# A fused attention and gated-MLP kernel on one core: the first phase's hand-written order is replaced, with 55 in place of 78 identity products in it

## The chip, the cores and the metric

The kernel runs on one core of a Trainium2 chip. A core has TensorE (matrix products), VectorE, ScalarE, GpSimd (POOL in the rows) and SyncE, whose queue here issues all DMA loads and stores. The metric is the device time of one execution in microseconds.

## The reference

Eight batches of eight heads have 576 positions of width 64. Keys and values are averaged over groups of 8 positions, so each head attends to 72 pooled keys. The result, with all heads side by side, is the input x of 4608 tokens of width 512 for a normalised gated MLP of inner width 1536. All arrays are float32 for the kernel (the weights arrive as float64).

```python
k_p = k.reshape(B, H, Sp, pool, D).mean(axis=3)      # pool = 8, Sp = 72
v_p = v.reshape(B, H, Sp, pool, D).mean(axis=3)
scores = scale * np.matmul(q, k_p.transpose(0, 1, 3, 2))
attn = np.exp(scores - max);  attn = attn / (sum + 1e-09)
x = (attn @ v_p), heads side by side                  # 4608 x 512
xn = x / sqrt(mean(x * x) + 1e-06) * rms_g
g = xn @ w_gate;  val = xn @ w_val                    # 512 -> 1536
out = (g * sigmoid(g) * val) @ w_out                  # 1536 -> 512
```

## The kernel before

**Tiling.** The tokens go in nine blocks of 512. Each factor of a large product is split in a high part and a rest, and three products are added (high × high, low × high, high × low), so one gate tile (f, one of 12 slices of 128 inner columns) takes 12 TensorE products of 512 columns, its value tile another 12, and its share of the output product 12 more.

**Two phases.** `later_phase` (from block 1 on) and `first_phase` each run a hand-written table of steps, `LATER` and `ORDER`. No planner stands behind it: the scheduler is in manual mode, and every engine and SyncE's queue take their instructions in the order in which the table names them. A step that waits holds up whatever follows on the same engine. `first_phase` loads and converts all weights, does the attention of batches 0 and 1, and block 0 of the MLP.

**The steps of the first phase** carry a letter and digits (base 36); after a colon stand the PSUM banks:

- `k`, `q`, `v` load keys, queries, values of a batch and a pair of heads; `K` (L360) and `V` (L369) pool them on VectorE. `S` is the scores (20 small products, L412), `M` the maximum (L378), `E` five exponentials on ScalarE (L390), `R` the inverse of the sums (L396), `N` the normalising on POOL (L402), `T` the transposes on TensorE (L472), `C` or `D` their copies out on VectorE (L478) or ScalarE, `A` the product with the values (L494), `X` or `Y` the copy of x on VectorE (L516) or ScalarE. `k`, `q`, `v` to `Y` have batch, pair and head or half as digits: T122 is batch 1, pair 2, third transpose group.
- For the norm of batch 0: `Z` squares (L521), `J` joins on POOL (L545), `P` sums over channels on TensorE (L587), `p` the total (L592), `r` the root (ScalarE, L599, with a table load), `s` its reciprocal (L602), `B` the spread over partitions (TensorE, L611), `H` the scaling (L619). `I`, `x`, `y` make block 0's scaled x (L827), its high part (ScalarE, L832) and its low part xl (VectorE, L837).
- Weights come in chunks, `l` to `w`, in the order that `CHUNKS` gives (chunk 8 is gate and value of f = 4, chunk c of f = 6, e of f = 7): `l` loads (L261), `a` takes the absolute value (ScalarE, L272), `b` shifts (L276), `c` ors in the low word (L280), `d` the sign (L284), on VectorE, `h` casts the high part (ScalarE, L298), `w` takes the rest (VectorE, L302). Raw loads of neighbouring slices alternate between two spaces (line 256), so the load of chunk c waits until chunk 8's `d` has read it.
- `g`, `e` are the gate and value products (L848), `G` the silu (ScalarE), `F` its product with the value (VectorE, L860), `i`, `j` the high part (ScalarE, L870) and the low part (VectorE, L878), `o` the output product (L892). `t` makes the part of block 1's x, `Q` squares batch 1's x.
- `z` is the identity product: `warm(n)` (L962) multiplies the identity with itself n times, and nobody reads the result. It stands between steps of TensorE, as in `zg:0` (16 of them) or `za:2` (10). In the trace such a product shows as two rows.

**Stages.** Four buffers (`st0` to `st3`) take the raw halves of the weight chunks, the transposes' copies, squares and later tiles. The string `STAGES` names for each tile, in the order of the program, which of the four it takes; a tile waits until the last reader of the former one is done.

Of the kernel before, what the change touches and what calls it, by code (L numbers as in the profile page):

```python
# [49 lines left out]


ORDER = """
k01 zg:0 q00 k00 K00 v00 q01 v01 q02 k02 v03 v02 k03 K01 za:7 S00:01 M000 M001 q03 l3 l1 E000 z2:7 S01:45 M010 E010
M011 E011 E001 V00 K02 zf:7 S02:06 R000 N000 R011 N011 z4:7 T011:1 T000:5 V03 M020 R001 N001 K03 z2:7 S03:32 M021 E020
R020 N020 C011 M030 C000 T001:1 C001 E021 R021 N021 R010 N010 M031 V01 E030 R030 N030 T002:0 D002 T020:4 C020 V02 a1
b1 z2:7 A000:1 Z00 A001:0 Z01 Y001 T021:5 z2:7 T022:0 E031 D022 Y000 R031 D021 z4:7 T030:4 c1 l0 a0 b0 d1 c0 z1:7
A020:1 Y020 Z20 D030 T010:0 D010 l2 a2 l5 k10 q10 l4 v10 z2:7 T012:1 C012 N031 T032:5 z2:7 A021:0 Y021 h1 Z21 J02 d0
T031:4 C031 w1 C032 A010:1 Z10 h0 K10 w0 z2:7 A011:0 Z11 A030:5 S10:46 M100 M101 a5 Y011 Y010 Z30 a3 E100 b2 b3 R100
b5 c2 A031:0 Z31 J01 P01:7 za:2 P03 p E101 c3 R101 N101 r0 s0 za:2 B00:1 a4 Y031 k11 X030 V10 N100 z2:2 T100:0 D100 I1
x1 c5 I0 x0 I3 I2 d3 d5 d2 y1 z4:2 T102:0 D102 x3 y0 T101:5 D101 h5 x2 y2 z4:2 A101:1 A100:0 y3 b4 g0:2 e0:3 h2 Y100  # L60
Y101 h3 w3 w2 l6 q11 v11 l7 a7 b7 l9 K11 S11:01 c4 G0 F0 d4 c7 a6 b6 d7 i0 h4 B01:4 w5 c6 H01 h7 j0 d6 g1:2 e1:3 G1 a9
F1 b9 w4 w7 c9 o0:4567 g2:2 lb l8 a8 b8 la ld i1 Q10 j1 o1 d9 e2:3 c8 d8 ab h6 G2 M111 bb M110 h8 w6 g3:2 V11 E110
R110 N110 T110:0 h9 w9 E111 F2 R111 N111 T111:1 i2 ad D110 k12 K12 v12 lc cb aa db D111 hb bd cd j2 dd ba w8 ca T112:0
e3:3 o2 G3 F3 ac hd D112 i3 wb da bc g4:2 e4:3 q12 lf lh le af bf k13 cf j3 A111:0 df ha wa wd V12 G4 F4 cc ae hf i4
ah wf A110:1 Y110 o3 g5:2 j4 o4 e5:3 be dc bh ch ce dh hc wc de G5 F5 v13 lj lg li aj Y111 bj Q11 J11 S12:01 M121 i5
j5 hh wh he M120 we cj dj g6:2 e6:3 ag G6 bg cg q13 ll lm o5 g7:2 E120 R120 N120 E121 R121 N121 F6 dg T120:1 hj i6 ai
bi V13 wj j6 ci al hg T121:0 C121 D120 K13 bl wg e7:3 lk ln G7 F7 T122:0 D122 o6 cl di dl i7 hi j7 A121:1 A120:0 Y120
wi X121 am bm ak bk g8:2 S13:01 M130 ck M131 hl wl E130 G8 R130 N130 dk E131 R131 N131 Q12 J12 an bn o7 e8:3 g9:2 F8
i8 j8 cn dn cm dm T130:1 T131:0 C130 hk G9 e9:3 o8 F9 wk D131 hn hm wm T132:0 D132 ga:2 A130:0 lp ap bp wn lo i9 j9
X130 cp dp A131:1 X131 Ga Q13 J13 ao ea:3 o9 Fa ia bo co do P10:0 r1 s1 ja hp wp gb:2 B10:0 H10 ho wo B11:1 H11 eb:3  # L70
oa Gb Fb t0 ib jb k20 v20 q20 t2 t3 t1 K20 V20 ob
"""


# [125 lines left out]
lo89 mo89 hi8a lo8a mo8a hi8b lo8b mo8b ev80 ev81 st80 st81 ev82 ev83 st82 st83  # L200
"""
STAGES = """
0123012301203102303213003213231201233102131221302121032130213231031323132113210302330113003210203210320120323013031201
01302321210231010102310312313032310321
"""
EXP_SCALE = 1.0 / (POOL * float(np.sqrt(D)))
# [790 lines left out]
```

## Time and profile before

| | us |
|---|---|
| median of 3 runs (1003.81 to 1010.04) | 1007.66 |
| profiled execution | 1005.87 |
| its span | 1004.0 |
| TensorE busy | 982.4 (98%) |
| VectorE busy | 672.7 (67%) |
| ScalarE busy | 475.6 (47%) |
| POOL busy | 201.7 (20%) |

The profile is of one execution, and the time of an instruction is read from its row: start, duration, engine, line, operation, tiles, and in brackets the idle time before it with what ended it. TensorE's clock is granted in full (1.00) or in part; its mean over this span is 0.997. Rows of consecutive instructions overlap a little, as one is started before the other's last writes are out.

### The profile page before, as it was taken

How to read it: one execution, taken by the hardware profiler on the slowest of the kernel's cores; microseconds unless marked ns; L12 is line 12 of the kernel's file. 1: busy time of each engine (PE TensorE's matmuls, PEld its weight loads, DVE VectorE, ACT ScalarE, POOL GpSimd, SP SyncE). 2: the span in 40 equal slices, each digit the busy share in tenths (PEclk: the TensorE clock that was granted, in tenths of full speed). 3: DMA queues.
4: the chain of work that ended last, by engine and by line, in shares of the span. 5: the costliest groups of instructions: out<-in, count | busy, mean ns of one | idle time of the engine just before them, and what ended most of it. 6: DMA issues, size and time to landing. Idle time of an engine off the chain costs nothing.

```text
span 1004.0 us, 13974 instructions
## 1 busy us (share of the span) xinstructions
PE 982.4 (98%) x4914; PEld 776.0 (77%) x4914; DVE 672.7 (67%) x1107; ACT 475.6 (47%) x865; POOL 201.7 (20%) x201
## 2 busy tenths in 40 slices
PE   9999999999899999899999999999999999999998
PEld 8877778777677778687777778788777787888886
DVE  6899977866776958467777788754567744444442
ACT  5867674655656644346575454632254321111221
POOL 2200111566545568201111020000010000000000
PEclk9999999999899999999999999999999999999999
DMA  9545511888666751668786661665565225545411
GB/s 280 175 148 197 197 43 60 251 248 257 210 204 213 227 184 63 212 187 237 205 232 188 200 191 48 200 191 154 149 177 140 73 95 153 152 147 147 148 42 42
DMA packets 115797, 167.35 MB, mean 167 GB/s; under 512 B 9552, under 2 KB 70992, under 8 KB 114448
## 3 DMA queue, kind: packets, MB, share of 16 engines
q1 hardware_dynamic: 115728, 166.47, 54.4%
q8 instruction: 39, 0.64, 0.3%
q14 instruction: 30, 0.25, 0.1%
HBM read 121.21 MB, written 45.22 MB: 166 GB/s over the span
## 4 chain that ended last, share of the span: by engine, by line
PE 79%; DVE 8%; ACT 4%; issue 3%; POOL 2%; DMA 2%; SPq 0%; ACTq 0%; POOLq 0%; DVEq 0%
PE po L892 25%; PE py L800 20%; PE px L800 15%; PE psg L848 12%; PE psx L494 3%; PE pss L412 3%; DMA main<-kT 1%; DVE hl L878 1%; ACT prob L390 1%; POOL wsum L709 1%; DMA sum<-wt 1%; DVE wt L284 1%; DVE act L860 1%; DVE xp L774 1%; POOL wt L722 1%
## 5 line engine op out<-in xcount | busy, mean ns | idle before, releaser
L892 PE MATMUL po<-w,hh 128*128 128x512 f32 x864 | 225.6, 390 | 0.0
L800 PE MATMUL py<-xp,wp 128*128 128x512 f32 x864 | 221.7, 392 | 1.6 <-DVE u L954 1.6
L800 PEld LDWEIGHTS py<-xp,wp 128*128 128x128 f32 x864 | 160.9, 188 | 39.4 <-DVE u L954 2.6
L892 PEld LDWEIGHTS po<-w,hh 128*128 128x128 f32 x864 | 161.9, 188 | 35.3 <-issue 1.2
L848 PE MATMUL psg<-xh,w 128*128 128x512 f32 x576 | 183.4, 400 | 4.3 <-DVE act L860 4.1
L800 PE MATMUL px<-xp,wp 128*128 128x512 f32 x648 | 166.4, 392 | 2.0 <-ACT act L949 1.9
L800 PEld LDWEIGHTS px<-xp,wp 128*128 128x128 f32 x648 | 120.4, 188 | 31.5 <-ACT act L949 3.4
L848 PEld LDWEIGHTS psg<-xh,w 128*128 128x128 f32 x576 | 106.6, 190 | 34.9 <-issue 6.7
L892 PE MATMUL po<-w,hl 128*128 128x512 f32 x432 | 125.0, 398 | 2.5 <-DVE hl L878 2.3
L848 PE MATMUL psg<-xl,w 128*128 128x512 f32 x288 | 113.3, 395 | 0.1
L443 POOL TENSOR_TENSOR prob<-prob,sm 128x360 f32<-128x360 f32 x48 | 40.5, 843 | 332.4 <-DVE sm L439 306.4
L892 PEld LDWEIGHTS po<-w,hl 128*128 128x128 f32 x432 | 79.0, 188 | 26.7 <-DVE hl L878 5.9
L878 DVE TENSOR_TENSOR hl<-act,hh 128x512 fp32r<-128x512 f32 x72 | 57.7, 801 | 30.9 <-ACT hh L870 28.4
L947 ACT COPY hb<-px 128x512 f32<-128x512 f32 x36 | 21.1, 587 | 110.5 <-PE px L800 110.5
L870 ACT CAST hh<-act 128x512 fp32r<-128x512 f32 x72 | 44.8, 622 | 58.7 <-DVE act L860 31.0
L950 DVE TENSOR_TENSOR u<-u,py 128x512 f32<-128x512 f32 x36 | 24.6, 683 | 67.6 <-PE py L800 67.6
L952 ACT ACTIVATE hb<-hb 128x512 f32<-128x512 f32 x36 | 22.7, 632 | 95.6 <-DVE hb L951 95.5
L848 PEld LDWEIGHTS psg<-xl,w 128*128 128x128 f32 x288 | 54.6, 190 | 12.7 <-DVE xl L837 0.9
L433 ACT ACT_TABLE_LOAD x38 | 48.8, 1283 | 0.7
L878 DVE TENSOR_TENSOR hl<-hb,hh 128x512 fp32r<-128x512 f32 x36 | 24.7, 687 | 34.3 <-ACT hh L870 34.3
L870 ACT CAST hh<-hb 128x512 fp32r<-128x512 f32 x36 | 22.4, 622 | 51.1 <-PE po L892 51.1
L722 POOL TENSOR_TENSOR wt<-wsum,wt 128x256 fp32r<-128x256 f32 x48 | 39.2, 820 | 35.2 <-ACT wt L718 35.2
(135 smaller groups left out, 1312.0 us busy)
## 6 DMA issues: line engine op xcount, KB each, us to landing
wp<-sum SPq DMA_DIRECT2D x144, 256.0 KB
wp<-blocks SPq DMA_DIRECT2D x108, 256.0 KB
sum<-wt SPq DMA_DIRECT2D x48, 256.0 KB
blocks<-w SPq DMA_DIRECT2D x24, 512.0 KB
wx<-w SPq DMA_DIRECT2D x10, 1024.0 KB
v<-vN SPq DMA_DIRECT2D x32, 288.0 KB
out<-o SPq DMA_DIRECT2D x36, 256.0 KB
wx<-w SPq DMA_DIRECT2D x16, 512.0 KB
```

Of the source, the lines that this page charges most:

```text
L412: nc.tensor.matmul(s["ps", h][:, t * SP:(t + 1) * SP], s["q"][r, o:o + P], s["pk"][r, :], start=True, stop=True)
L433: nc.scalar.activation(l_pr(h), l_pr(h), AF.Exp, scale=EXP_SCALE)
L443: nc.gpsimd.tensor_tensor(l_pr(h), l_pr(h), sm[:, :, None].broadcast_to([P, len(OFFS2), SP]), ALU.mult)
L494: nc.tensor.matmul(ps[r, :n], s["pv"][:, r], x, start=True, stop=True)
L722: nc.gpsimd.tensor_sub(y[:, 1], place(f, f"T{k}"), y[:, 0].bitcast(F32))
L800: nc.tensor.matmul(ps[:, :NB], w[:, a, c, :], x[:, b, c, :], start=j == 0 and not more, stop=j == len(todo) - 1, skip_group_check=more)
L848: nc.tensor.matmul(ps[:, :NB], w[:, c, cols], x[c], start=(j == 0), stop=(j == len(todo) - 1))
L870: nc.scalar.copy(a, act_in(i, f))
L878: eng.tensor_sub(l, act_in(i, f), hh[i, f].bitcast(F32))
L892: nc.tensor.matmul(po[i, t], x[i, f][:, t * P:(t + 1) * P], w, start=(f == 0 and k == 0), stop=(f == NF - 1 and k == 2))
L950: u3=lambda i, f: V.tensor_add(u3(i), u2(i), st["Y", i, f, 3]),
L952: sw=lambda i, f: S_.activation(later(i, f), later(i, f), AF.Silu),
```

## The change

The table `ORDER` is written anew, with the same steps but for the identity products (16 at the start and 55 after them, in place of 16 and 78), and the copies out of the transposes and of x divided slightly differently over VectorE and ScalarE. The first 20 characters of `STAGES` give other buffers to the tiles from chunk b on. `LATER` and all functions stay as they are. The first line of the table and the string:

```diff
 ORDER = """
-k01 zg:0 q00 k00 K00 v00 q01 v01 q02 k02 v03 v02 k03 K01 za:7 S00:01 M000 M001 q03 l3 l1 E000 z2:7 S01:45 M010 E010
...
+zg:0 k01 q00 k00 v00 K00 S00:01 K01 q01 v01 z1:7 S01:45 q02 k02 v03 v02 k03 q03 l3 M000 E000 l1 l0 V00 M010 M011 E011
...
 STAGES = """
-0123012301203102303213003213231201233102131221302121032130213231031323132113210302330113003210203210320120323013031201
+0123023102310232131203103213231201233102131221302121032130213231031323132113210302330113003210203210320120323013031201
```

TensorE around the sum over channels (psr, lines of `P`) and the spread of the root (psb), before:

```order
L494 MATMUL psx_3_1_498<-own_254 64x288 x2
L587 MATMUL psr_503<-one,own_127 116x1 x5
L962 MATMUL warm<-ident 128x128 x10
L587 MATMUL psr_503<-one,own_254 116x1 x5
L962 MATMUL warm<-ident 128x128 x10
L611 MATMUL psb_0_550<-ident,r_536 128x116 x3
```

and in the changed kernel:

```order
L494 MATMUL psx_3_1_457<-own_246 64x288 x2
L962 MATMUL warm<-ident 128x128 x2
L587 MATMUL psr_469<-one,own_127 116x1 x5
L962 MATMUL warm<-ident 128x128 x10
L587 MATMUL psr_469<-one,own_246 116x1 x5
L962 MATMUL warm<-ident 128x128 x13
L611 MATMUL psb_0_528<-ident,r_511 128x116 x3
```

Thirteen identity products stand ahead of the spread in place of ten, and two more ahead of the first sum.

VectorE from the reciprocal of the root (r) to the first low part of block 0's x (xl); pv and pk are pooled values and keys of batch 1, xraw is x, wt a weight chunk under conversion. Before:

```order
L602 RECIPROCAL r_536<-r_536 116x5
L516 COPY xraw_346<-psx_3_0_460 128x288
L369 TENSOR_REDUCE pv_0_562<-v_0_412 72x128
L827 SCALAR_TENSOR_TENSOR xraw_346<-xraw_346,gcol,psb_0_550 128x512
L280 SCALAR_TENSOR_TENSOR wt_480<-wx_404,wt_480 128x512
L827 SCALAR_TENSOR_TENSOR xraw_346<-xraw_346,gcol,psb_0_550 128x512 x3
L284 SCALAR_TENSOR_TENSOR wt_485<-wx_158,wt_485 128x512
L284 SCALAR_TENSOR_TENSOR wt_480<-wx_404,wt_480 128x512
L284 SCALAR_TENSOR_TENSOR wt_402<-wx_400,wt_402 128x1024
L837 TENSOR_TENSOR xl_1_587<-xraw_346,xh_1_576 128x512
```

and in the changed kernel:

```order
L602 RECIPROCAL r_511<-r_511 116x5
L369 TENSOR_REDUCE pv_0_547<-v_0_545 72x128
L276 TENSOR_SCALAR wt_549<-wt_549 128x1024
L360 TENSOR_REDUCE pk_1_554<-k_1_552 128x72
L827 SCALAR_TENSOR_TENSOR xraw_338<-xraw_338,gcol,psb_0_528 128x512 x4
L276 TENSOR_SCALAR wt_567<-wt_567 128x1024
L837 TENSOR_TENSOR xl_0_591<-xraw_338,xh_0_589 128x512
```

The four steps of x stand in one run; one low word and three signs have gone from between them and xl, and a pool of keys and two shifts have come in ahead of xl.

TensorE at the transposes of batch 1, pair 2 (pst_2) and tile f = 7 (psg_7_0 gate, psg_7_1 value; po is the output product of f = 6), before:

```order
L848 MATMUL psg_7_0_1181<-xl_3_625,w_7_1124 128x512
L472 MATMUL pst_2_0_1213<-ident,prob 72x128 x4
L472 MATMUL pst_2_1_1235<-ident,prob 72x128 x4
L848 MATMUL psg_7_1_1246<-xh_0_580,w_7_1124 128x512 x2
...
L848 MATMUL psg_7_1_1246<-xl_3_625,w_7_1124 128x512
L472 MATMUL pst_2_2_1266<-ident,prob 72x128 x2
```

and in the changed kernel:

```order
L848 MATMUL psg_7_1_1170<-xl_3_605,w_7_1061 128x512
L472 MATMUL pst_2_1_1216<-ident,prob 72x128 x4
L472 MATMUL pst_2_0_1228<-ident,prob 72x128 x4
L472 MATMUL pst_2_2_1234<-ident,prob 72x128 x2
L892 MATMUL po_0_716<-w_6_1105,hl_6_1200 128x512
```

All three groups of transposes stand behind the value tile of f = 7, and the second group goes first.

Elsewhere in the table, among others: N110 (the normalising of batch 1, pair 1, first head) stands ahead of o1, e2 and g3, and the transposes T110, T111 and T112 behind g3; M130 and M131 stand next to each other; the second spread (B01) stands ahead of g0 in place of behind S11; and the sign step `d8` stands behind K12, close ahead of the load `lc`:

```
before:  ... e2:3 c8 d8 ab h6 G2 ... D110 k12 K12 v12 lc cb ...
after:   ... db G2 E110 R110 N110 o1 e2:3 g3:2 c8 F2 h9 E111 R111 V11 k12 w9 K12 d8 v12 lc ...
```

## Rows read from the trace of the kernel before

**Rows 1.** The page's account of the chain that ended last: shares of the span by engine.

```profile
PE 79%; DVE 8%; ACT 4%; issue 3%; POOL 2%; DMA 2%; SPq 0%; ACTq 0%; POOLq 0%; DVEq 0%
```

**Rows 2.** Busy time in stretches of 25 us: stretch, its length, then busy time and count of instructions of TensorE, its weight loads, VectorE, ScalarE and POOL, the granted clock, the share of the DMA engines and GB/s.

```profile
50.00:75.00 25.00, 24.59 (x120) 19.06 (x119) 24.90 (x37) 16.28 (x24) 0.00 (x0) 1.00 0.41 152
75.00:100.00 25.00, 23.21 (x109) 18.10 (x108) 23.68 (x37) 17.62 (x41) 2.07 (x2) 1.00 0.59 197
100.00:125.00 25.00, 23.27 (x123) 18.53 (x123) 23.88 (x35) 16.80 (x40) 3.56 (x3) 1.00 0.52 199
```

**Rows 3.** TensorE's timeline where it stood idle in the first phase, and its last row (start, duration, instruction, in brackets the idle time before it and what ended it).

```profile
63.08 1.17 PE L892 MATMUL po<-w,hl 128*128 128x512 f32 x4 [0.16 <-DVE hl L878]
...
78.11 0.63 PE L472 MATMUL pst<-ident,prob 128*72 128x128 f32 x4 [0.92 <-POOL prob L402]
79.61 0.85 PE L472 MATMUL pst<-ident,prob 128*72 128x128 f32 x6 [0.88 <-POOL prob L402]
...
121.41 0.41 PE L472 MATMUL pst<-ident,prob 128*72 128x128 f32 x2 [1.74 <-DVE pt L478]
...
140.02 0.63 PE L472 MATMUL pst<-ident,prob 128*72 128x128 f32 x4 [0.70 <-POOL prob L402]
140.90 0.74 PE L848 MATMUL psg<-xh,w 128*128 128x512 f32 x2 [0.25 <-DVE act L860]
...
169.58 0.61 PE L892 MATMUL po<-w,hh 128*128 128x512 f32 x2
```

**Rows 4.** TensorE's timeline, the opening and the way to the second gate tile.

```profile
18.68 0.61 PE L962 MATMUL warm<-ident 128*128 128x128 f32 x4
20.12 1.34 PE L412 MATMUL pss<-own,main 64*128 64x72 f32 x20 [0.84 <-DVE own L360]
...
36.32 1.18 PE L587 MATMUL psr<-one,own 128*116 128x1 f32 x10 [0.17 <-POOL own L545]
...
40.61 2.48 PE L962 MATMUL warm<-ident 128*128 128x128 f32 x20
42.93 1.22 PE L611 MATMUL psb<-ident,r 116*128 116x116 f32 x10
...
49.18 2.14 PE L848 MATMUL psg<-xh,w 128*128 128x512 f32 x8
...
52.65 0.63 PE L848 MATMUL psg<-xh,w 128*128 128x512 f32 x2
...
55.70 1.34 PE L412 MATMUL pss<-pk,q 64*128 64x72 f32 x20
56.97 0.43 PE L611 MATMUL psb<-ident,r 116*128 116x64 f32 x2
57.21 0.70 PE L848 MATMUL psg<-xh,w 128*128 128x512 f32 x2
```

**Rows 5.** VectorE's timeline: opening, root, x and its low part, and two places further on.

```profile
19.27 0.75 DVE L360 TENSOR_REDUCE own<-main 128x72 f32<-128x576 f32 x1 [0.48 <-DMA main<-kT]
...
40.79 0.17 DVE L592 TENSOR_REDUCE total<-psr 116x5 f32<-116x10 f32 x1 [0.42 <-PE psr L587]
...
42.40 1.21 DVE L369 TENSOR_REDUCE pv<-v 72x128 f32<-72x1024 f32 x1
44.18 0.75 DVE L827 SCALAR_TENSOR_TENSOR xraw<-xraw,gcol,psb 128x512 f32<-128x512 f32 x1 [0.57 <-PE psb L611]
...
45.45 2.06 DVE L827 SCALAR_TENSOR_TENSOR xraw<-xraw,gcol,psb 128x512 f32<-128x512 f32 x3
47.42 2.42 DVE L284 SCALAR_TENSOR_TENSOR wt<-wx,wt 128x512 uint32<-128x512 uint32 x3
49.76 2.49 DVE L837 TENSOR_TENSOR xl<-xraw,xh 128x512 fp32r<-128x512 f32 x4
52.17 0.69 DVE L276 TENSOR_SCALAR wt<-wt 128x1024 uint32<-128x1024 uint32 x1
...
88.22 1.03 DVE L276 TENSOR_SCALAR wt<-wt 128x1024 uint32<-128x1024 uint32 x2
...
141.53 0.69 DVE L878 TENSOR_TENSOR hl<-act,hh 128x512 fp32r<-128x512 f32 x1 [0.69 <-ACT hh L870]
```

**Rows 6.** ScalarE's timeline around copies and weight chunks, and the issues of loads on SyncE's queue (SPq).

```profile
79.12 0.59 ACT L478 COPY pt<-pst 72x512 f32<-72x512 f32 x1
...
84.87 1.16 ACT L272 ACTIVATE wt<-wx 128x1024 f32<-128x1024 f32 x1 [0.40 <-DVE w L302]
...
93.26 1.16 ACT L272 ACTIVATE wt<-wx 128x1024 f32<-128x1024 f32 x1 [1.97 <-DMA wx<-w]
...
75.89 0.33 SPq L261 DMA_DIRECT2D wx<-w  x1
...
76.75 11.96 SPq L261 DMA_DIRECT2D wx<-w  x3
```

**Rows 7.** TensorE and VectorE around 251 us, and the busy time of two microseconds from 254 us (columns as in rows 2).

```profile
254.49 1.22 PE L848 MATMUL psg<-xh,w 128*128 128x512 f32 x2 [2.91 <-DVE act L860]
...
259.91 0.90 PE L494 MATMUL psx<-pt,pv 72*64 72x256 f32 x4
...
246.92 6.92 DVE L578 SCALAR_TENSOR_TENSOR xraw<-xraw,gcol,acc 128x288 f32<-128x288 f32 x8
...
254.00:256.00 2.00, 1.51 (x4) 1.24 (x5) 1.97 (x5) 1.52 (x2) 0.00 (x0) 0.50 0.96 283
```

More of the change, by code (lines that the diff above doesn't have):

```diff
@@ L52 @@
 ORDER = """
-k01 zg:0 q00 k00 K00 v00 q01 v01 q02 k02 v03 v02 k03 K01 za:7 S00:01 M000 M001 q03 l3 l1 E000 z2:7 S01:45 M010 E010
[L54 to L71, printed above, removed]
+zg:0 k01 q00 k00 v00 K00 S00:01 K01 q01 v01 z1:7 S01:45 q02 k02 v03 v02 k03 q03 l3 M000 E000 l1 l0 V00 M010 M011 E011
@@ new lines @@
+l2 l5 k10 q10 R000 N000 M001 E001 K02 zf:7 S02:06 E010 T000:5 R011 N011 T011:1 V03 M020 E020 K03 z1:7 S03:32 R001 M021
+E021 N001 T002:0 C011 M030 R020 N020 E030 C000 T001:1 C001 D002 M031 E031 R030 R021 N021 z4:7 T020:4 C020 V02 N030
+R010 N010 z1:7 A001:0 Z01 Y001 R031 N031 A000:1 Z00 V01 a1 b1 c1 z1:7 T021:5 T022:0 D022 Y000 D021 a0 b0 T030:4 D030
+A020:1 Z20 Y020 T010:0 D010 a2 c0 d0 z2:7 T012:1 C012 d1 A021:0 Z21 T031:4 C031 K10 T032:5 C032 Y021 h1 w1 h0 w0
+A010:1 Z10 Y010 A011:0 Z11 l4 S10:46 M100 b2 M101 Y011 a5 b5 c2 A030:5 Z30 A031:0 J02 J01 a3 b3 Z31 z2:2 P01:7 za:2
@@ new lines @@
+P03 p X030 E100 R100 c3 E101 R101 N101 d3 r0 s0 zd:2 B00:1 Y031 N100 z2:2 T100:0 v10 V10 a4 b4 k11 K11 I2 l6 q11 v11
+D100 I0 I1 I3 a6 b6 z3:2 T102:0 D102 T101:5 D101 B01:4 A100:0 x0 y0 x1 y1 x2 y2 Y100 x3 y3 h3 w3 A101:1 Y101 g0:2 e0:3
+G0 d2 h2 c6 c5 l7 a7 w2 d6 h6 F0 i0 c4 b7 d4 h4 H01 j0 c7 S11:01 M111 d7 g1:2 e1:3 h7 G1 w4 d5 F1 o0:4567 g2:2 Q10 w7
+h5 w5 i1 j1 l9 a9 lb l8 la ld a8 w6 b9 c9 ab bb M110 cb b8 d9 db G2 E110 R110 N110 o1 e2:3 g3:2 c8 F2 h9 E111 R111 V11
+k12 w9 K12 d8 v12 lc q12 aa i2 j2 ba T110:0 D110 ad bd h8 w8 N111 T111:1 D111 ca cd da T112:0 D112 G3 e3:3 o2 g4:2 F3
@@ new lines @@
+dd ac bc cc hb hd wd wb A110:1 A111:0 Y110 i3 j3 Y111 e4:3 lf af bf V12 cf G4 ha wa o3 g5:2 lh le k13 F4 ae i4 dc j4
+o4 v13 df ah bh be ce K13 de ch hc wc e5:3 G5 F5 dh he we lj lg li S12:01 M121 i5 M120 j5 q13 ll lm ag bg hh wh cg dg
+hf ai bi wf aj bj cj g6:2 G6 e6:3 F6 o5 dj g7:2 e7:3 E121 R121 N121 E120 al i6 j6 bl hj wj hg Q11 R120 N120 cl J11
+T121:0 C121 G7 F7 wg ci di T120:1 D120 T122:0 D122 lk ln ak bk o6 ck dl i7 am j7 A121:1 X121 V13 bm A120:0 Y120 hi wi
+hl g8:2 G8 o7 Q12 J12 S13:01 M130 wl M131 dk E130 cm R130 E131 R131 an bn cn hk e8:3 F8 g9:2 dn hn wn i8 j8 N131
@@ L72 @@
+T131:0 D131 N130 T130:1 C130 e9:3 o8 T132:0 G9 dm hm D132 F9 i9 wk ga:2 A130:0 wm X130 A131:1 X131 lp ap lo ao bo Q13
+j9 bp ea:3 o9 Ga cp dp Fa ia hp k20 v20 K20 ja co do J13 P10:0 r1 s1 gb:2 B10:0 H10 B11:1 Gb ho H11 eb:3 wo oa Fb ib
+jb wp t2 t0 t3 t1 V20 ob q20
 """
```

## The prediction

> **What bounds the kernel now.** I read the chain of waits first [rows 1]: TensorE is 79% of it, VectorE 8%. Time is won where TensorE stands idle, or is busy with something that nobody reads. The change touches only the first phase, whose last out product on TensorE ends at 170.1 (169.58 and on [rows 3]). So the second view is TensorE's busy time in stretches of 25 us [rows 2]: from 50 to 125 us it lacks 0.4, 1.8 and 1.7 of them, with VectorE at 24.90, 23.68 and 23.88 of 25. Both are nearly full, and single places decide. The third view, TensorE's timeline with its gaps, names them [rows 3]: 0.16 (63.08), 0.92 (78.11), 0.88 (79.61), 1.74 (121.41), 0.70 (140.02), 0.25 (140.90). Up to about 50 us TensorE hides its idle time under identity products; there I follow the chain that lets the first gate product start, on TensorE [rows 4] and VectorE [rows 5].
>
> The profiled execution took 1005.87 us, 1.79 under the median of 1007.66. The sum is made against the first. Rows overlap by some 0.08; a cost in a queue is taken from start to start.
>
> **Opening: no gain.** The loads that go first keep their order, and VectorE's pool of k03 starts at 19.27, when its load lands [rows 5]; S03 starts at 20.12 [rows 4]. The chain behind it (exponentials, transposes, squares, J01) keeps its instructions on their engines, so I carry P01 over at 36.3.
>
> **Root and spread: +0.65.** 10 products stood between the sums P03 and the spread B00, at 2.32 (40.61 to 42.93 [rows 4]); now 13, 3 × 0.232 = 0.70. On VectorE X030 (0.35), two inverses (0.6), a low and a sign (1.2) now stand between the total p, at 40.79 [rows 5], and the reciprocal s0, which comes at about 43.0 and so not behind the products. B00 starts at 43.6 in place of 42.93.
>
> **First gate product (A): −1.45.** VectorE waited 0.57 for B00 and ran, from 44.18, an x (0.66) and a low (0.60), from 45.45 three more x, from 47.42 three signs (2.34) and from 49.76 four xl (0.60 each), the last ending at 52.2 [rows 5]. In the changed order V10 (1.13, as at 42.40), a shift (0.60, as at 52.17) and K11 (0.66, the size of the row at 19.27) fill the time from 43.05, so the four x begin at 45.45: 4 × 0.66, a shift 0.60, four xl at 0.60, end 51.1. That is 1.1 earlier though x begins later, because the low and the signs no longer stand between. The gate's 12 products had waited on the xl from inside: 49.18 to 52.65, 3.5, where the value's 12 took 3.0 up to S11 at 55.70. Now 51.1 + 0.3 for the last xl product + 3.0 + S11's 1.27 = 55.7. B01's 0.24, ahead of the next gate before (57.21), goes ahead of the first. The weights of that next gate end on VectorE behind a half w, a sign, two lows and a w (512 words 0.60, 1024 words 1.13): 51.1 + 0.60 + 1.13 + 1.13 + 0.60 + 1.13 = 55.7. So g1 starts at 55.75: −1.45.
>
> **T110 and T111 (B): −1.5.** They waited 0.92 and 0.88 for POOL's normalise [rows 3]. Now o1, e2 and g3, 12 products each and over 8 us together, run between the normalise of N110 and T110. Both gaps go, and so does the 0.16, since j0 stands ahead of S11's maximum. Next late is T112, which needs T110's bank copied out by ScalarE (D110, 0.59 as at 79.12 [rows 6]): I leave 0.45. 0.16 + 0.92 + 0.88 − 0.45 = 1.5. Bounds of the new wait: 0, and the 1.74 that a transpose waited for such a copy.
>
> **T122 (C): −1.44.** It waited 1.74 for C121, behind conversions on VectorE [rows 3]. Now all three transposes stand behind e7, 12 products later, and I leave 0.3: the copy less the transposes beside it. Bounds again 0 and 1.74.
>
> **T131 and e9 (D): +0.15.** 0.70 and 0.25 before. M130 and M131 stand together and the order of the transposes turns: N131 comes 0.75 late by the queues, N130 0.35. ScalarE loads two tables fewer, as the exponentials of both heads stand side by side; its idle time covers that.
>
> Sum on TensorE: **−4.25**, its part of the phase ends near 165.9.
>
> **Loads and POOL.** Chunks lb to lo and batch 1's squares take other stage buffers. The only load that the queue issues clearly later is lc (below). The later phase keeps its order; its first POOL step, a sum of weights that block 3 wants, shares its buffer with v20 before and with a square now. It can start earlier; I cost it at nothing, its cover being the time until block 3.
>
> **What is carried to the end.** At 251.58 TensorE waits 2.91 for VectorE (a value product behind eight scale steps that start at 246.92), and the clock then stands at 0.50 from 254 on [rows 7]. That wait ends on VectorE, so what counts there is VectorE's lead. Behind the last value product VectorE has Fb, jb, wp, the pairs of t and V20: jb waits about 0.69 for ScalarE's hi, as at 141.53 [rows 5], which a t covered before. With 0.1 to 0.2 from wp in K20's place the lead is 3.4 there and 4.25 on TensorE. I take **−3.8**, between them. 1005.87 − 3.8 = 1002.1; by medians 1007.66 − 3.8 = **1003.9**. With B's and C's waits 0.8 off either way: 1002.2 to 1005.2.
>
> **The rivals.**
>
> *The clock falls in the opening.* Two products (18.68) and a gap of 0.84 stood ahead of S03 [rows 4], and four more ahead of the transposes before. Now one stands there, and with S02 and two transposes done by 17.4 TensorE has nothing until 20.0: 2.6. Rows: gaps of 0.84 to 1.74 left the clock at 1.00, one of 2.91 halved it [rows 3, 7], and 2.6 is nearer to that. Price: S03's 20 rows (1.34) at half speed, +1.3, up to +2.5 with the transposes behind them; they feed ScalarE's queue, which hands it on to J01. Then 1005.2 to 1006.4. The Trainium skill, "TensorE: Matmul & The Clock Gate", Part 1, says "the default state is throttled, and activity releases the throttle"; by that rule products that nobody reads are worth something, and the sum would be this rival's 1005.8. The trace agrees at 254.
>
> *A load that comes too late* (slower). Load lc goes into the space that chunk 8 leaves with its sign step d8. Before, d8 stood early, and lc was issued at 75.89 [rows 6]. Now d8 stands behind K12 on VectorE: about 78.2. Its data are wanted by ac on ScalarE and then by bc on VectorE, which stood at 88.22 [rows 5] and comes at about 84.95 by A, B and its place. One landing is bounded from below by le's: the last of three issues (76.75 and 11.96 on), so at 88.4, read at 93.26 after a wait for the transfer: 4.9. lc at 83.1 is in time. From above: lc itself, read at 84.87 after an issue at 75.89, 9.0. Then lc lands at 87.2, ac ends at 88.25, VectorE's queue moves by 3.3 and o3 with it. A stall of 3.3 is longer than the one that halved the clock, which cost 2.7 more (12 products from 254.49 to 259.91 in place of 2.7). −3.8 + 3.3 + 2.7 = +2.2: **1009.9**. It decides from 6 us of landing on.
>
> *The gap at 251 closes.* If later transfers find their place earlier, both the 2.91 and the slow 2.7 go: 998.3. Against it: both engines move together.
>
> *It is swallowed.* If VectorE's steps up to 246.92 hang on transfers and not on its own queue, the gap grows by what was won: 1007.7. For it: the second batch's loads share the time. Against it: the scale steps run without a break, 6.92 for eight [rows 7].
>
> **Chances.** Forecast 0.50, clock 0.20, late load 0.13, closed gap 0.07, swallowed 0.10. The range leaves out most of the late load and half of the closed gap: **998.5 to 1009.5**. A measurement of this kernel tells some 1%, 10 us, from no change: faster by that 0.06 (the closed gap and more behind it), slower 0.04 (the late load and a second stall), the same 0.90.
>
> **What would show it.** In the changed profile: four x in one row from 45.4, the last xl ending at 51.1, g1 at 55.75 (A); no gaps ahead of T110 and T111, e3 at 77.2 in place of 80.22 (B); under 0.5 ahead of T122 (C); the phase's last out product ending near 165.9, and the wait of about 2.9 near 247. A granted clock under 1.00 from 6 to 24 us shows the first rival, ScalarE waiting for a transfer near 85 us the second. I am wrong in the main if the first gate's chain is not shorter, or if T112 and T122 wait as long as T110 and T121 did.

## The result, and the profile after

| us | before | after |
|---|---|---|
| median of 9 runs each (lowest to highest) | 1005.82 (1003.21 to 1010.04) | 1014.19 (1012.27 to 1016.59) |
| profiled execution, its span | 1005.87, 1004.0 | 1015.59, 1013.6 |
| TensorE busy | 982.4 | 981.2 |
| POOL busy | 201.7 | 211.1 |

The ratio is 1.009, with an interval of 1.0072 to 1.0108: the change makes the kernel 8.4 us **slower**, 0.9%. The forecast was 1003.9, and the time lies outside the range too. Three single executions among all the runs took far longer than the others of their kernel (1103.66 to 2498.27), and medians and ratios leave them out. One row of the small table is odd: POOL executes the same work and is busy for 9.4 us more.

The chain of waits after, as shares of the whole span, and then some of its pieces from 72 to 93 us (start, duration, instruction):

```profile
PE 79%; DVE 8%; ACT 4%; POOL 3%; DMA 3%; issue 2%; SPq 1%; ACTq 0%; POOLq 0%; DVEq 0%
...
76.15 9.55 POOL prob L402
...
85.74 1.49 PE pst L472 x6
87.23 4.86 PE psg L848 x12
```

The shares hardly move against [rows 1]. The pieces name the loss: one POOL step, the normalise N111, takes 9.55. POOL's timeline of both kernels, first before, then after:

```profile
78.77 0.79 POOL L402 TENSOR_TENSOR prob<-prob,mx 128x360 f32<-128x360 f32 x1 [0.72 <-ACT hh L870]
```

```profile
74.14 1.58 POOL L402 TENSOR_TENSOR prob<-prob,mx 128x360 f32<-128x360 f32 x1 [28.75 <-ACT w L298]
76.15 9.54 POOL L402 TENSOR_TENSOR prob<-prob,mx 128x360 f32<-128x360 f32 x1 [0.43 <-DVE mx L397]
...
146.42 2.27 POOL L402 TENSOR_TENSOR prob<-prob,mx 128x360 f32<-128x360 f32 x2 [5.45 <-ACT wt L272]
```

The same instruction on the same shapes takes 0.79 in one order and 9.54 in the other. TensorE's timeline after shows who pays:

```profile
56.48 0.73 PE L848 MATMUL psg<-xh,w 128*128 128x512 f32 x2
...
62.06 1.07 PE L892 MATMUL po<-w,hl 128*128 128x512 f32 x4
...
75.77 0.63 PE L472 MATMUL pst<-ident,prob 128*72 128x128 f32 x4
85.74 1.49 PE L472 MATMUL pst<-ident,prob 128*72 128x128 f32 x6 [9.33 <-POOL prob L402]
86.88 1.20 PE L848 MATMUL psg<-xh,w 128*128 128x512 f32 x2
...
91.93 1.07 PE L892 MATMUL po<-w,hl 128*128 128x512 f32 x4
...
128.33 0.92 PE L472 MATMUL pst<-ident,prob 128*72 128x128 f32 x6 [0.28 <-POOL prob L402]
...
147.55 0.63 PE L472 MATMUL pst<-ident,prob 128*72 128x128 f32 x4 [1.35 <-POOL prob L402]
148.75 0.63 PE L472 MATMUL pst<-ident,prob 128*72 128x128 f32 x4 [0.56 <-POOL prob L402]
...
180.35 1.34 PE L412 MATMUL pss<-pk,q 64*128 64x72 f32 x20
...
266.04 1.22 PE L848 MATMUL psg<-xh,w 128*128 128x512 f32 x2 [2.90 <-DVE act L860]
```

The gap ahead of T110 (0.92 in [rows 3]) is gone, and that ahead of T111 is 9.33 in place of 0.88. Then the clock is down. Two microseconds behind the stall (columns as in [rows 2]):

```profile
88.00:90.00 2.00, 2.00 (x6) 1.53 (x5) 0.00 (x0) 1.99 (x3) 0.00 (x0) 0.50 0.97 400
```

At 0.50, the lower of its two levels, the 12 products of e3 take 5.05 (86.88 to 91.93); before they took 2.85 (80.22 to 83.07), so the stall costs 2.2 more behind itself, and another 0.5 in the six transposes ahead of them (1.14 for 0.61 from start to start). VectorE, which was full in [rows 2], waits too; its timeline at the first xl and over the stall:

```profile
48.94 2.55 DVE L837 TENSOR_TENSOR xl<-xraw,xh 128x512 fp32r<-128x512 f32 x4 [0.30 <-ACT xh L832]
...
75.81 0.19 DVE L397 RECIPROCAL mx<-mx 128x5 f32<-128x5 f32 x1
75.92 1.17 DVE L369 TENSOR_REDUCE pv<-v 72x128 f32<-72x1024 f32 x1
77.01 0.68 DVE L302 TENSOR_TENSOR w<-wt,w 128x512 fp32r<-128x512 f32 x1
77.61 0.74 DVE L360 TENSOR_REDUCE pk<-k 128x72 f32<-128x576 f32 x1
78.28 1.21 DVE L284 SCALAR_TENSOR_TENSOR wt<-wx,wt 128x1024 uint32<-128x1024 uint32 x1
79.41 0.68 DVE L878 TENSOR_TENSOR hl<-act,hh 128x512 fp32r<-128x512 f32 x1
80.01 1.02 DVE L276 TENSOR_SCALAR wt<-wt 128x1024 uint32<-128x1024 uint32 x2
80.95 1.22 DVE L302 TENSOR_TENSOR w<-wt,w 128x1024 fp32r<-128x1024 f32 x1
82.08 1.82 DVE L280 SCALAR_TENSOR_TENSOR wt<-wx,wt 128x1024 uint32<-128x1024 uint32 x2
83.82 1.21 DVE L284 SCALAR_TENSOR_TENSOR wt<-wx,wt 128x1024 uint32<-128x1024 uint32 x1
92.20 0.69 DVE L860 TENSOR_TENSOR act<-act,psg 128x512 f32<-128x512 f32 x1 [7.17 <-PE psg L848]
```

The inverse that N111 needs is done at 76.0. From 75.92 to 85.03 VectorE runs eleven steps without a break, and N111 ends at 85.69, 0.66 after the last of them. The row doesn't show when POOL worked; its end suggests that most of its 0.79 of work was done when VectorE had stopped.

### The profile page after: what moved, and what is told of

It is laid out like the page before. It is cut to its first block, busy times and chain, and to the rows that moved or that the text cites. A ratio compares the mean times of both kernels' runs of the same rounds, so it can differ in the third digit from the quotient of the medians.

```text
span 1013.6 us, 13874 instructions
## 1 busy us (share of the span) xinstructions
PE 981.2 (97%) x4868; PEld 774.3 (76%) x4868; DVE 676.7 (67%) x1107; ACT 472.4 (47%) x863; POOL 211.1 (21%) x201
## 4 chain that ended last, share of the span: by engine, by line
PE 79%; DVE 8%; ACT 4%; POOL 3%; DMA 3%; issue 2%; SPq 1%; ACTq 0%; POOLq 0%; DVEq 0%
PE po L892 25%; PE py L800 19%; PE px L800 14%; PE psg L848 13%; PE psx L494 3%; PE pss L412 3%; POOL prob L402 1%; DMA v<-vN 1%; DMA out<-o 1%; DVE hl L878 1%; DVE w L302 1%; ACT prob L390 1%; DVE wt L280 1%; DVE act L860 1%; DVE wt L284 1%
## 5 line engine op out<-in xcount | busy, mean ns | idle before, releaser
L722 POOL TENSOR_TENSOR wt<-wsum,wt 128x256 fp32r<-128x256 f32 x48 | 42.2, 882 | 36.2 <-ACT wt L718 36.1
L860 DVE TENSOR_TENSOR act<-act,psg 128x512 f32<-128x512 f32 x36 | 24.6, 683 | 33.5 <-PE psg L848 31.1
```

Source lines behind the costliest of these rows:

```text
L722: nc.gpsimd.tensor_sub(y[:, 1], place(f, f"T{k}"), y[:, 0].bitcast(F32))
L860: nc.vector.tensor_mul(t, t, ps[:, :NB])
```

## The experiments

Theory from here on, **port**: a POOL step cannot run beside certain VectorE steps, and an unbroken run of them keeps it out. The Trainium skill, "SBUF — State Buffer", Who interferes with whom, states such a rule: the two engines share one pair of ports, a VectorE step with two inputs in SBUF (the on-chip memory that holds the tiles) "contends with a GpSimd instruction that reads SBUF", and a `tensor_reduce` does not. The rival, **input**: N111 waits for something else that the profile doesn't show, so moving VectorE's steps would not help.

**N111 on VectorE.** The same inverse, the same product, another engine:

```diff
-... E111 R111 V11
+... E111 R111 n111 V11
...
-... h8 w8 N111 T111:1 ...
+... h8 w8 T111:1 ...
...
+... n=lambda b, p, h: s_norm(b, p, h, V), ...
```

> Theory (SBUF port): in the changed kernel POOL's normalise N111 took 9.54 us in place of 0.79 because VectorE, without a break beside it, kept it from the memory; T111 waited 9.33 for it and the clock halved for the 12 products of e3 (5.0 in place of 2.7). With N111 on VectorE right behind R111 (0.5 us more there) the gap ahead of T111 is under 1, e3 starts at 77 to 78 in place of 86.9, and the whole takes 1014.2 - 9.3 - 2.3 + 0.5 = about 1003, within 0.5% of the kernel before. Rival (a late weight load, or ScalarE, holds the whole group up and POOL's row only shows it): the gap ahead of T111 or e3 stays above 5 us, time above 1009.

Measured: 1003.96 (1000.45 to 1008.85), ratio 0.9988 (0.9965 to 1.0012). The gap ahead of T111 is 0.38, under 1 as expected. TensorE's timeline:

```profile
75.09 0.60 PE L472 MATMUL pst<-ident,prob 128*72 128x128 f32 x4 [0.38 <-DVE prob L402]
```

**Both pools of VectorE directly behind the inverse.** Only w9 and K12 change places:

```diff
-k12 w9 K12 d8 v12 lc ...
+k12 K12 w9 d8 v12 lc ...
```

> One swap in the changed kernel: K12 (a reduction, one input) ahead of w9 (a subtraction of two tiles), N111 stays on POOL. Theory, port taken step by step: behind R111 stand two reductions, 1.8 us without a two-input step, N111 (0.79) runs in 0.8 to 1.0 beside them, the gap ahead of T111 goes, about 1003. Rival 1 (POOL is slow beside any unbroken run of VectorE): N111 takes 9 us again, about 1014. Rival 2 (a load or ScalarE): no change either, 1014, with POOL's row at 9.

Measured: 1003.46 (1000.5 to 1007.3), ratio 0.998 (0.9961 to 0.9999). POOL's timeline, and VectorE's:

```profile
76.42 0.79 POOL L402 TENSOR_TENSOR prob<-prob,mx 128x360 f32<-128x360 f32 x1 [0.43 <-DVE mx L397]
```

```profile
76.18 1.18 DVE L369 TENSOR_REDUCE pv<-v 72x128 f32<-72x1024 f32 x1
77.28 0.74 DVE L360 TENSOR_REDUCE pk<-k 128x72 f32<-128x576 f32 x1
77.94 0.68 DVE L302 TENSOR_TENSOR w<-wt,w 128x512 fp32r<-128x512 f32 x1
```

N111 runs in 0.79 beside a reduction, and the gap ahead of T111 is 0.59. One swap of two VectorE steps gives the whole loss back (a ratio of 0.998 for 1.009); input falls, since no input of N111 moved.

**The subtraction w9 ahead of V11**, directly behind the inverse, so that two reductions follow it:

```diff
-... R111 V11 k12 w9 K12 d8 ...
+... R111 w9 V11 k12 K12 d8 ...
```

> The changed kernel with w9 ahead of V11: the two-input step is the first behind R111, two reductions follow. If the port is given step by step, N111 waits for w9 (0.6) and runs beside the reductions: 1.4 to 1.6, ending near 77.5; gap ahead of T111 about 1.3, about 1004. If a POOL step that has once lost the port stays out until VectorE rests, N111 takes 9 again and the time is about 1014.

Measured: one run of 1002.9; N111 takes 1.07, under the expected 1.4 to 1.6, and the gap ahead of T111 is 0.87. So a POOL step that loses one VectorE step need not stay out until VectorE rests.

**A bench ahead of the unchanged new order.** 14 POOL steps of N111's form, each followed by VectorE steps that nobody reads; it adds their time, so only its rows count:

```diff
...
+        tests = [[], [red, tt, tt, tt, tt, tt, tt], ..., [tt] * 8, [stt] * 8, [sh] * 8, [red] * 5,
+                 [pt] * 8, ..., [red2, stt, stt, stt, stt, stt, stt]]
...
+        for ops in tests:
...
+            V.reciprocal(sm[:, :n], sm[:, :n])
...
+            G.tensor_tensor(x, x, sm[:, :n, None].broadcast_to([P, n, SP]), ALU.mult)
+            for op in ops:
+                op()
...
```

> Ahead of the kernel before's successor stand 14 unread tests: a normalise on POOL of the size of N111 on scratch tiles, released by the same two tiny steps of VectorE, beside a run of VectorE steps of one kind. Theory: alone 0.8; beside 8 two-input steps in SBUF (subtract, or shift-or) 4.8 + 0.8 = 5.6 or more; beside 5 reductions or 8 steps with one input in PSUM 0.8; beside 8 shifts of one tile 0.8 or, if these hold the port too, over 5. One reduction and then 6 subtractions: 0.8 if the port is given step by step in the order of need, 1.1 + 3.6 + 0.7 = 5.4 if a subtraction that stands next takes it already. Rival (nothing with the port): all 14 take 0.8 to 1.5.

POOL's timeline of six tests: alone, a pool of values (`red`) and six subtractions, eight subtractions, five pools of values, eight products with a PSUM input, and a pool of keys (`red2`) and six shift-ors:

```profile
13.60 0.79 POOL L1004 TENSOR_TENSOR bpr<-bpr,bsm 128x360 f32<-128x360 f32 x1 [12.29 <-DVE bsm L1002]
14.96 2.19 POOL L1004 TENSOR_TENSOR bpr<-bpr,bsm 128x360 f32<-128x360 f32 x1 [0.58 <-DVE bsm L1002]
...
41.60 1.07 POOL L1004 TENSOR_TENSOR bpr<-bpr,bsm 128x360 f32<-128x360 f32 x1 [3.59 <-DVE bsm L1002]
...
60.89 0.79 POOL L1004 TENSOR_TENSOR bpr<-bpr,bsm 128x360 f32<-128x360 f32 x1 [5.37 <-DVE bsm L1002]
67.28 0.79 POOL L1004 TENSOR_TENSOR bpr<-bpr,bsm 128x360 f32<-128x360 f32 x1 [5.61 <-DVE bsm L1002]
...
84.12 0.79 POOL L1004 TENSOR_TENSOR bpr<-bpr,bsm 128x360 f32<-128x360 f32 x1 [4.15 <-DVE bsm L1002]
```

Reductions and PSUM inputs leave POOL at 0.79; subtractions, and likewise shift-ors and shifts, make it 1.07; a pool of values with a subtraction or a shift-or next makes it 2.19. The classes agree with the Trainium skill's rule, but for the shifts, which have one input and are not covered by what is quoted. That the pool of values delays POOL when a two-input step stands next, and not when a second reduction does (0.79), comes from these rows alone; with the shorter pool of keys ahead of shift-ors it stayed at 0.79. The expected 5.6 beside eight subtractions is missed by far (1.07): POOL was held up by one step, not by all eight. And nothing here lasts 9: the N111 of the kernel itself, later in the same execution, again took 9.54.

**Is it VectorE's order alone? Before's order with V11 and w9 behind R111:**

```diff
-... g3:2 V11 E110 R110 N110 T110:0 h9 w9 E111 F2 R111 N111 T111:1 ...
+... g3:2 E110 R110 N110 T110:0 h9 E111 F2 R111 V11 w9 N111 T111:1 ...
```

> The kernel before, with V11 and w9 moved behind R111, as they stand in the changed one; nothing else. Theory (N111 starved at this place by these two steps): N111 takes 8 to 10 us in place of 0.79, the gap ahead of T111 becomes 8 to 10 in place of 0.88, the clock halves for the group behind it, and the time is 1005.1 + 8 to 11, about 1014. Rival (it takes the rest of the changed order too, its loads or its ScalarE queue): gap under 2, 1004 to 1007.

Measured: 1007.07, ratio 1.0024 (1.0006 to 1.0043). N111 takes 2.38, not 8 to 10: a miss. The gap ahead of T111 is 2.96. Something near the bench's 2.19 is met again, the long stall is not.

**Four-word clears between R111 and V11**, one, then four, in the changed order; nothing else moves:

```diff
-... E111 R111 V11
+... E111 R111 n1 V11
...
+n=lambda m: [V.memset(dots[:, :4], 0.0) for _ in range(m)]
```

> The changed kernel with one unread 4-word clear on VectorE (some 0.06 us) between R111 and V11; w9 stays where it is. Theory (whether N111 gets in is decided by when its request comes against the steps that already stand in VectorE's queue): N111's request falls at or before V11's start; it may still lose (9 us, about 1014) or win (0.8, about 1003). Rival (the steps themselves decide, whenever the request comes): 9 us, 1014. Only a short N111 tells them apart.

> The same with four clears, some 0.3 us: N111's request now comes ahead of V11's start, with nothing of two inputs running or next. Theory (arrival decides): N111 takes 0.8 to 1.1, gap ahead of T111 under 1, about 1003. Rival (the run of V11, w9, K12 and the two-input steps behind decides): 8 to 10 us, about 1014.

POOL's timeline with one clear, and with four:

```profile
74.74 9.58 POOL L403 TENSOR_TENSOR prob<-prob,mx 128x360 f32<-128x360 f32 x1 [0.43 <-DVE dots L931]
```

```profile
76.36 0.79 POOL L403 TENSOR_TENSOR prob<-prob,mx 128x360 f32<-128x360 f32 x1 [0.43 <-DVE dots L931]
```

One clear: 1012.02. Four clears: 1003.68. These are single runs, but the profiles show the wait ahead of T111 at 9.38 and at 0.58: three more clears in VectorE's queue decide over 8.8 us of it. With four, N111 starts 0.19 ahead of V11 (76.36 and 76.55); with one, 0.22 behind it (74.74 and 74.52). In pools_first it started 0.24 behind V11 and took 0.79 all the same, so both the moment and the steps behind V11 count.

**A forced rest of VectorE.** Nine small copies on ScalarE, and one VectorE copy that waits for them, stand between the shifts and w8:

```diff
-... ad bd h8 w8 N111 ...
+... ad bd h8 m9 n1 w8 N111 ...
...
```

> The changed kernel with a forced rest of VectorE in the middle of its run: nine unread 64-column copies on ScalarE behind the cast h8, and one unread 4-word copy on VectorE that waits for them, between the shifts and w8. Theory (N111 is out until VectorE rests): VectorE idles for 0.5 to 1.5 us from about 5 us after N111's start, and N111 ends some 0.7 after that rest begins: it takes 5 to 6 in place of 9.54, the gap ahead of T111 is 5 to 6 in place of 9.33, time 1008 to 1011. Rival (N111 waits for something that ends only after the whole run, or simply takes 9.5): N111 takes 9.5 or more.

POOL's and VectorE's timelines:

```profile
75.23 5.53 POOL L405 TENSOR_TENSOR prob<-prob,mx 128x360 f32<-128x360 f32 x1 [0.43 <-DVE mx L400]
```

```profile
79.10 1.02 DVE L279 TENSOR_SCALAR wt<-wt 128x1024 uint32<-128x1024 uint32 x2
82.04 0.17 DVE L934 COPY dots<-wide 128x4 f32<-128x4 f32 x1 [1.93 <-ACT wide L933]
```

The rest begins at 80.1 (82.04 − 1.93), and N111 ends at 80.76, 0.65 later; behind the unbroken run it ended 0.66 later. The gap ahead of T111 is 5.33, and the one run took 1011.98, a little over the expected 1008 to 1011. This is the cleanest row for port: the end of N111 follows the moment at which VectorE stops.

**The step behind K12.** d8, and the load lc that it frees, go behind j2, so that j2, another two-input step, follows K12 in d8's place:

```diff
-k12 w9 K12 d8 v12 lc q12 aa i2 j2 ba ...
+k12 w9 K12 v12 q12 aa i2 j2 d8 lc ba ...
```

> The changed kernel with d8 (and the load lc that waits for it) behind j2, so that what follows V11, w9 and K12 is j2, which waits for ScalarE's cast, in place of d8, which waits for nothing. If what keeps N111 out is d8, ready to run while K12 does, N111 takes 1.5 to 2.5, as in the kernel before with the same two steps ahead, and the time is about 1004. If any two-input step behind K12 does it, 8 to 10 and about 1014.

Measured: N111 takes 2.37 and the gap is 2.17, as expected if d8 is what keeps N111 out; but the one run took 1009.08 (1006.67 before on that chip), where about 1004 was expected. VectorE had no break at this point either: j2 starts at 76.72, when K12 ends. So the step that stands directly behind K12 matters, and a two-input step there is not enough for the long stall.

**Four more benches**, with the eleven VectorE steps of the kernel in their order, a busy VectorE ahead, eight moments of the request, or TensorE and ScalarE beside them:

> Ahead of the order with K12 pulled forward stand 17 unread tests of one POOL step beside VectorE runs on scratch: the normalise on contiguous or on 96-word rows, and the weight step of the later phase, beside the very 11 steps that follow R111 in the changed kernel, and beside parts of them. In the first bench no POOL step was out for more than one two-input step (at most 2.19). Theory 1 (the sequence does it: a reduction over 72 partitions, a subtraction, a reduction, then two-input steps without a break): the 11 real steps give 8 to 10 on either layout, and the same without the leading reduction 0.8 to 2. Theory 2 (the layout of POOL's operand does it): 8 to 10 on the 96-word rows alone, also beside 8 subtractions. Rival (it takes the state of the real program: loads, ScalarE, semaphores): no test over 2.5.

> 18 unread tests as in the second bench, now with VectorE busy (two steps of 1024 words and one from PSUM) right up to the two tiny steps that release POOL. In the second bench VectorE had stood idle before, and the 11 real steps kept POOL out for 2.25 only. Theory (a busy VectorE has its next two-input steps already in line, so POOL loses at every end of a step): the 11 real steps behind a busy VectorE give 8 to 10; five clears between give 0.8 to 1.1; a reduction behind a reduction gives 0.8. Rival (VectorE's past does not count): the same values as in the second bench, 2.2 for the 11 steps, 1.1 for eight subtractions.

> 32 unread tests: the normalise on POOL, released by a ScalarE copy of 8 to 456 columns and so at eight moments some 0.05 us apart, beside ten subtractions of 512 words, the 11 real steps, six shift-or steps of 1024 words, ten subtractions of another tile. In the three earlier benches no POOL step lost more than two ends of a step, in the changed kernel it lost nine in a row. Theory (whether POOL gets in at the end of a step depends on the moment at which its request falls into the step that runs): for most moments 0.8 to 1.4, for one or two of the eight, those late in a step, 5 or more, until VectorE rests. Rival (the moment does not matter, the real program's own state does): every test between 0.8 and 2.9.

> Nine unread tests of the POOL normalise beside the 11 real steps, with the real program's surroundings added one by one: identity products on TensorE, ScalarE copies, a ScalarE step that feeds the subtractions, a ScalarE step that reads each result, and all together behind a busy VectorE. Theory (one of these surroundings makes POOL lose every time): 2.2 alone, and 8 to 10 from the test on that adds it. Rival (none of these): 1.6 to 2.9 in all nine.

None brought the long stall: the longest POOL step in them was 2.86, and the kernel's own steps in their order gave at most 2.26. The expectations that one of these would bring it all failed. What the kernel has and the benches lack, so that N111 stays out over eleven VectorE steps, is **open**.

**Do the identity products matter?** Before's order with 23 of them taken out:

```diff
-... K01 za:7 S00:01 ... E000 z2:7 S01:45 ... K03 z2:7 S03:32 ...
+... K01 S00:01 ... E000 z1:7 S01:45 ... K03 z1:7 S03:32 ...
...
```

> The kernel before with 23 identity products fewer (10 ahead of S00, one ahead of S01, 4 and 1 ahead of T011 and S03, 7 among the transposes), 71 in all as in the changed kernel. Theory (those products hide TensorE's idle time only): granted clock 1.00 all through the opening, P01 at 36.3 and the first gate product at 49.2 as before, time within 0.2% of 1005.1. Rival (the clock falls in the opening): clock under 1.00 between 6 and 24 us, P01 1.3 to 2.5 later, about 1007.

Measured: 1004.93, ratio 0.9998 (0.9973 to 1.0024). Its profiled execution took 1011.57, with the clock down in the opening (columns as in [rows 2]):

```profile
20.00:22.00 2.00, 2.00 (x18) 1.78 (x17) 1.50 (x5) 1.60 (x11) 0.79 (x1) 0.50 1.05 425
30.00:60.00 30.00, 29.60 (x186) 24.41 (x184) 22.53 (x43) 20.01 (x52) 5.03 (x4) 0.83 0.36 123
```

The median doesn't move, as expected; but the clock was not at 1.00 all through the opening, and the profiled execution took 6.6 more than the median.

**The better order.** Onto the swap of w9 and K12, the value step vl17's place in the later phase, so that its VectorE step stands between eight scale steps:

```diff
-wf40 rs21 wh41 wl41 vl17 mx310 ...
+wf40 vl17 rs21 wh41 wl41 mx310 ...
```

> The order with K12 pulled forward, and in the later phase the value product of block 1's slice 7 moved from behind the eight scale steps to between the two groups of four (VectorE only). Theory (the wait of 2.91 near 251 is VectorE's queue): the wait goes or falls under 0.5, and with it, in the runs in which the clock halves there, 2.7 more: 0.994 to 0.996 of the kernel before, about 1000. Rival (the scale steps are late themselves, the next group waits for them): the wait comes back behind, 0.998.

Measured: 1000.93 (998.33 to 1004.39), ratio 0.9946 (0.9928 to 0.9965). VectorE's and TensorE's timelines:

```profile
248.64 3.79 DVE L578 SCALAR_TENSOR_TENSOR xraw<-xraw,gcol,acc 128x288 f32<-128x288 f32 x4
252.35 0.67 DVE L860 TENSOR_TENSOR act<-act,psg 128x512 f32<-128x512 f32 x1
252.95 2.77 DVE L578 SCALAR_TENSOR_TENSOR xraw<-xraw,gcol,acc 128x288 f32<-128x288 f32 x4
```

```profile
20.05 2.41 PE L412 MATMUL pss<-own,main 64*128 64x72 f32 x20 [2.10 <-DVE mx L396]
...
256.83 0.65 PE L494 MATMUL psx<-pt,pv 72*64 72x256 f32 x4 [0.73 <-PE psg L848]
```

The wait of 2.91 [rows 7] is gone. But this execution shows a gap of 2.10 ahead of S03, and S03 takes 2.41 for the 1.34 of [rows 4]: the clock was 0.50 there. So the gap is filled with eight unread products more:

```diff
-... K03 z1:7 S03:32 R001 ...
+... K03 z9:7 S03:32 R001 ...
```

> The kernel of both (K12 forward, the value product between the scale steps) with nine identity products in place of one ahead of S03 (2.1 us, in the gap of some 2 us in which TensorE waits for K03). In the profiled executions of this order the clock fell to 0.50 at 20 to 24 us in four of nine, at 1.5 to 2 us each. Theory (the gap ahead of S03 makes it fall): the clock stays at 1.00 from 6 to 30 us, S03 starts no later, and the median is 0.5 to 1 us under that of both, 0.993 to 0.995 of the kernel before. Rival (the gaps between the transposes do it, or the landing of k03): clock under 1.00 again, 0.995.

Measured: **998.78** (997.42 to 1000.96), ratio 0.9937 (0.9918 to 0.9956), the fastest of all and the least spread. Its interval overlaps with that of "both" (0.9928 to 0.9965), so what the eight products alone are worth is not shown. TensorE's timeline in the opening:

```profile
16.61 2.17 PE L962 MATMUL warm<-ident 128*128 128x128 f32 x18
18.71 1.34 PE L412 MATMUL pss<-own,main 64*128 64x72 f32 x20
```

## Why the prediction was wrong, step by step

**The step that failed is "T110 and T111 (B)".** It said "Both gaps go" and costed N111 at nothing, under the cover of o1, e2 and g3 on TensorE. The cover concerns TensorE; what decided was the engine beside POOL. In its new place N111 stands behind an inverse that VectorE follows with nine microseconds of its own steps without a break. It took 9.54 for 0.79, TensorE waited 9.33, far over the upper bound of 1.74 that the prediction gave the new wait, and e3 started at 86.88 for the 77.2 that was forecast. Without the 9.33 it would have started at 77.55. The half clock made it 2.2 more on e3. The prediction said itself that a VectorE full to 24.9 of 25 was one of two nearly full engines, and did not ask what that does to a POOL step on the path.

With this one loss taken away, by the swap or by moving the normalise, the kernel takes 1003.46 or 1003.96, and the forecast was 1003.9. That is nearer than the forecast deserves: those runs stand against a before of 1005.13, so the gain is 1.2 to 2.0 and not 3.8. The forecast started from 1007.66, a median of three; nine runs gave 1005.82. The other terms tell the rest, by starts on TensorE.

- **First gate product (A): mis-sized.** g1 starts at 56.48, not 55.75: −0.73 for −1.45. The last xl ends at 51.5 (48.94 + 2.55), 0.4 later than reckoned, since VectorE waited 0.30 for ScalarE's high part of x ahead of it. But the last xl no longer sets the start: TensorE shows no wait from 47.96 to 56.48. The gate's products start at 49.55 (49.18 before), and the four on xl take 0.90 from start to start, without a wait, for the 1.50 of before (51.15 to 52.65); the sum had 0.3 for them behind the last xl.

```profile
49.55 2.11 PE L848 MATMUL psg<-xh,w 128*128 128x512 f32 x8
51.50 1.07 PE L848 MATMUL psg<-xl,w 128*128 128x512 f32 x4
```

- **T110 and T111 (B) with the stall gone: nearly right.** With the swap T111 waits 0.59, where 0.45 was left.
- **T122 (C): right in size, by another wait.** The 0.28 stands ahead of T120 and ends on POOL's normalise N120; T122 runs directly behind it and waits for no copy. That it meets the 0.3 that was left for the copy is luck.
- **T131 and e9 (D): mis-sized.** The waits are 1.35 for T131 and 0.56 for T130, none for e9, against 0.70 and 0.25: +0.96 for +0.15. The clock is at 0.50 again at 150 us, and e9's 12 products take 4.43 for 2.89. N131 and N130 take 2.27 for two at 0.79, which fits the same contention at a smaller size. With the swap alone the waits are 1.06, 0.30 and 0.52 for e9.
- **What is carried: right in kind, mis-sized.** The wait near 251 stays, 2.90 for 2.91. S20 comes 10.22 late (170.13 before), the last wait of [rows 7] 11.55 late, the execution ends 9.72 late. From S20 to the end of that wait the new order takes 1.3 longer than the old, with the swap too (168.50 to 254.11 for 170.13 to 254.49); the forecast had allowed up to 0.85 for this (3.4 of 4.25).
- **Opening: right in the profiled execution** (the clock stayed at 1.00 there). The first rival, "The clock falls in the opening", is nevertheless real in others: in four of the experiments' profiles on the new order the clock went down to 0.50 behind S03. It fell where the gap ahead of S03 was 1.73 to 2.29; in the changed kernel's own profile that gap was 0.51, and in the other experiments' on this order, the benches aside, 1.37 at most. The gap's length alone does not tell: in the old order with fewer products the clock fell behind gaps of 1.05 and 0.44, and the wait of 2.91 near 251, behind which it had stood at 0.50 before, left it at 1.00 in the profiles of pools_first and norm_on_vector. Its price is inside the spread of the runs: "filled" is 2.2 under "both" by medians, which the intervals do not tell apart. The Trainium skill's rule that the prediction quoted, activity releases the throttle, fits the one profile of "filled", where the clock stayed at 1.00; that the products won time is not shown.
- **"A load that comes too late"** can't be seen in the changed kernel, because the stall gave the load time: ac runs at 89.39, 9.8 after the issue of lc. With the stall gone its sign is there, small. In pools_first lc is issued at 79.81, for the 78.2 that was reckoned, lands some 4.9 later, which is the lower bound of the prediction, and ScalarE waits for it:

```profile
84.72 1.15 ACT L272 ACTIVATE wt<-wx 128x1024 f32<-128x1024 f32 x1 [1.33 <-DMA wx<-w]
```

TensorE shows no wait behind it there.

- **The other two rivals.** The gap near 251 did not close. Of a lead to be swallowed the changed kernel had none; with the swap S20 comes 1.63 early and that wait ends 0.38 early, so most of this lead was lost on the way, by the 1.3 above.
- **A slip in the sum.** With both waits 0.8 off either way the narrower range is 1002.3 to 1005.5, not 1002.2 to 1005.2; nothing hangs on it.

What is shown: the loss comes from N111 on POOL (norm_on_vector), hangs on VectorE's steps beside it (pools_first, four_dots), and ends when VectorE rests (rest). What is only argued: that the shared ports of the Trainium skill's rule are the cause; the bench's two-input steps, reductions and PSUM inputs agree with it. Open is why N111 was kept out over eleven steps here, and in the benches over two or three.

## What to carry to other kernels

Before a POOL step goes onto a path, look at what VectorE runs from the moment at which its input is ready: put reductions, PSUM reads or a rest behind the step that releases POOL, or give VectorE the small step. A duration taken from a row holds only beside the neighbours that the row had. Where TensorE has a gap ahead of a chain and the clock falls behind it, unread products in the gap are worth a trial; what they win here is not shown.

## What the runs showed that was not expected

A POOL step of 0.79 can take any of 0.79, 1.07, 2.19, 5.53 or 9.54, with nothing changed but what stands beside it. One clear of four words left it at 9.58, four clears brought 0.79. It seems to work the other way too: beside POOL's N131 and N130, which start at 146.42, VectorE's shift-or at 146.89 takes 1.16 for 0.68.
